# A segmented memory-attention and gated-FFN kernel: the order and the buffers of its work written out as two tables

## Chip, cores and metric

The kernel runs on one core of one Trainium2 chip. The metric is the device time of one execution in microseconds (us), lower is better. Engines are named as in the profile: PE (TensorE matmul), PEld (TensorE weight load), DVE (VectorE), ACT (ScalarE), POOL (GpSimd), SP (SyncE, which issues most DMAs).

## The reference

Inputs are bf16: `x` of 2048 tokens by 512, four 512x512 attention matrices, a 32-vector `beta`, the FFN matrices (512x1792 twice, 1792x512) and a gate vector `gate_w`. Cut to what matters:

```python
q, k, v = heads(x @ wq), heads(x @ wk), heads(x @ wv)     # 32 heads of 16, 4 segments of 512
phi = lambda t: where(t > 0, t + 1, exp(t))
mask = (ar[:, None] < ar[None, :]) * -1e9
for s in range(4):
    p = softmax(qs @ ks.T * scale + mask)
    a_dot = p @ vs
    a_mem = (phi(qs) @ M) / (phi(qs) @ z + 1e-6)
    outs.append(sigmoid(beta) * a_mem + (1 - sigmoid(beta)) * a_dot)
    M = M + phi(ks).T @ vs
    z = z + phi(ks).sum(tokens)
a = concat(outs) @ wo
b = (relu(x @ W_gate) * (x @ W_up)) @ W_down
g = sigmoid((x * gate_w).sum(-1))
return g * a + (1 - g) * b
```

## The kernel before

A program on the host builds a list of 1331 tasks. Each task (`plan.add(engine, duration, key, emit, deps, ...)`) has an engine, the tasks it depends on, the buffers it needs (`need`) and frees (`frees`), and a function `emit` that writes its instructions. After the list is built, `Plan.run` puts all tasks into one order, and the last lines of the kernel call `emit` task by task. Each engine executes its own instructions in that order; the waits between engines follow from the data and the buffers. So the order decides who waits for whom, and the assignment of buffers decides which earlier reader a writer has to wait for.

In the kernel before, `Plan.run` is a list scheduler: it keeps a model time for every engine, and at each moment starts the ready task with the smallest key whose buffers are free. The keys are formulas over the segment and chunk, to which a table `SHIFT` adds an offset for most of the 1331 tasks. `SWITCH`, `BLOCK`, `PHASE`, `FETCH`, `COLX`, `LOOK` are parameters of that model.

The work is tiled into 4 segments (`seg`) of 512 tokens, each with 4 chunks (`c`) of 8 heads; unit `u` is 4 seg + c.

- `x0_tasks` transposes the first segment's rows on PE (12 + 4 flips); the other segments' `xT` come by transposing DMAs.
- `gate_tasks(seg)` computes the token gate: four products with accumulation on DVE (the line that the trace calls L610) over the rows `xn` of that segment, an exp on ACT (`rcol`), then ratios in two layouts. `xn` is one buffer: `load_xn(seg + 1)` (issued by SP, L480) may start only when the four products of `seg` are done. For segments 1 to 3 the ratios travel through DRAM (`ratio`, `rq`, `rtok`, `rr`). For segment 0, a DVE product `q0` and a small PE matmul with a constant `fold` spread them over the partitions.
- `proj_q`, `proj_k`, `proj_v` project one chunk (matmuls of 128x512, line L663; in a form with four column tiles, L667). DVE or ACT evict each PSUM bank (`QT` L752, `ktr` L768, `Vp` L798). `proj_k` then makes `KT` (three scalings, L771), `pkT` by phi (L727, L728, after an exp on ACT, L732) and the transpose `pK` by a DMA.
- `fill_vm(seg)` copies rows of `Vp` into `Vm` by two DMAs (L807).
- `attention(seg, c)`: four groups of scores on PE (L823), each filling PSUM banks 0 to 3, one exp of 128x2048 on ACT (L845) and a triangular mask on POOL (L874); `diag` for every second chunk (L836, L856); two PV groups on PE (L896); `normalise` (transposes L927, reciprocal L935, products L937 and L932, transpose L908) into `oT`.
- `memory`, `dens`, `recall` keep and read M and z (`mbd`, `omr` L988, `coefs` and `cdr` by DMA).
- `ffn_tasks`: 14 column blocks `fv` of gate (ACT relu into `rgr`, L1047) and up (DVE product into `hT`, L1053); then `out_tile` adds W_down and wo products for 128 tokens in one bank, DVE evicts with the factor 1 - g (`osr`, L1075), SP stores. The last token tile (`tt` 15) is done in two halves of 256 columns.

Rings limit how far work runs ahead: 14 `hT`, 6 `E`, 5 `QT`/`KT`/`pqT`, 3 `ktr`, `ex1`, `rgr`, 4 `pkT`, 2 `osr`, and 8 PSUM banks.

The set-up loads (`xn` of segment 0, wq, wk, wv, gate and up in four pieces, `xT(1)`, W_down, wo, `xT(2)`) are emitted before any task, so they come first on SP in every order. wq comes in two halves of 256 columns.

The order's last step reads:

```python
    for n, d in SHIFT.items():
        plan.tasks[n].key += d
    order = plan.run()
    for t in order:
        if t.emit is not None:
            t.emit(t.col) if t.flex else t.emit()
```

Of the kernel before, what the change touches and what calls it, by code (L numbers as in the profile page):

```python
# [8 lines left out]
F32 = mybir.dt.float32  # L9
# [3 lines left out]
P = 128  # L13
S = 2048
D = 512
# [10 lines left out]
SWITCH = 105.0  # L26
BLOCK, PHASE, FETCH = 256, 191, 2950.0
COLX = 4.0
DEFER = None
LOOK = 1000.0  # L30
# [4 lines left out]
SHIFT = {  # L35
    0: -25684, 1: 1407, 2: -1330, 3: -22978, 4: -30607, 6: 36389, 7: -5637, 8: -6641, 9:
    -9156, 10: 6383, 11: -4187, 12: -13726, 13: 12497, 14: 57538, 15: -5422, 16: 1476, 17:
    -21591, 18: 23771, 19: -4129, 20: -7981, 21: 280, 22: 7068, 25: -318, 28: 21268, 29:
    -15341, 30: -57736, 31: -21028, 32: -2196, 33: -8016, 34: -783, 35: -1107, 36: -633, 38:
    15, 40: 42372, 41: 65840, 42: 5113, 43: -71216, 44: 19414, 45: 21758, 47: 5746, 50: 654,  # L40
    51: 20403, 52: 53629, 53: -20631, 54: 7059, 55: -21405, 56: -13895, 57: -740, 58: -5913,
    59: -13897, 60: 1353, 61: -40120, 62: 24385, 63: -14621, 65: 25112, 66: 3543, 67: -38939,
    69: 6399, 71: -26793, 72: -4691, 73: -2524, 75: 40537, 76: -4748, 77: -586, 80: -1662, 81:
    -105183, 82: -62163, 83: -64288, 84: 18468, 85: -40339, 86: 37103, 87: -37065, 89: 8422,
    90: 16643, 91: -13637, 92: -14487, 93: -5073, 94: 1505, 96: -1554, 97: -747, 98: -9522,
    99: -4680, 100: 4639, 101: -97803, 102: 16395, 103: 38252, 104: -69147, 105: -10415, 106:
    27259, 107: -31419, 108: 13377, 109: -123574, 111: -12785, 112: -2378, 113: 3673, 114:
    -29140, 115: 4266, 116: -62363, 117: 88, 119: -4261, 121: -33231, 122: 9814, 123: 2110,
    125: 19178, 126: 17796, 127: -23382, 128: -6689, 129: -747, 130: 22411, 131: -31402, 132:
    -16511, 133: -1373, 134: -1496, 135: 8763, 136: 29491, 137: -749, 138: 29552, 139: -20100,  # L50
    140: 44658, 141: -80409, 142: -3139, 143: -26909, 144: 1803, 145: 386, 146: 16247, 147:
    65537, 148: -3529, 149: -6241, 150: 65653, 151: 46999, 153: 14030, 154: 44020, 155: 14760,
    156: 43561, 157: -7096, 158: 45936, 159: -26024, 160: 23457, 161: 50979, 162: -46625, 163:
    -54482, 164: 88981, 165: -28687, 166: -9744, 167: 114272, 168: -31967, 169: 9267, 170:
    38917, 171: -13229, 172: 5693, 173: -28492, 174: 3768, 177: 340, 178: -26186, 179: -31211,
    181: -31531, 182: 39351, 183: -15341, 184: -100921, 185: 22252, 186: -1779, 187: -3708,
    189: -4467, 191: 37936, 192: -46874, 193: 73026, 194: -5245, 196: 16791, 197: 4743, 198:
    -45159, 199: -43211, 200: -20335, 201: 1213, 202: 125, 203: 797, 204: 8260, 205: -173671,
    206: -2254, 207: 2086, 208: -44938, 209: 42530, 210: 2685, 211: -40581, 212: 31594, 213:
    -29665, 214: -2192, 215: -61393, 217: 4901, 218: 62, 219: -31560, 220: 8015, 221: -19756,  # L60
    222: -10130, 223: -18144, 224: 68794, 225: -54104, 226: -17099, 227: 38555, 228: 53992,
    229: -20805, 230: 2476, 231: -36425, 232: -2988, 233: -4667, 234: -11209, 235: 1392, 236:
    -22096, 237: -41776, 238: -415, 239: 1533, 240: 386, 241: 10244, 242: 16354, 243: -68385,
    244: 1929, 245: -59988, 246: -4306, 247: -23793, 248: -103183, 249: -2675, 250: 35079,
    251: 580, 253: -493674, 254: -20933, 255: 697, 256: -72948, 257: -3646, 258: -15000, 259:
    2471, 260: -20761, 261: -743, 262: 7412, 263: 20962, 264: 1114, 265: -5477, 266: 29635,
    267: -95694, 268: 15975, 269: -918, 270: -11522, 271: -41685, 272: 41485, 274: -239341,
    275: -1143, 276: -1006, 277: -1966, 278: -1511, 279: -68031, 280: 21386, 281: 115009, 283:
    -13976, 285: -26218, 286: 8903, 287: 24823, 288: 3414, 289: 51471, 290: 44714, 291: 65457,
    292: -5775, 293: 23342, 294: -52538, 295: 42735, 296: 28700, 297: -891, 298: 169, 299:  # L70
    -16564, 300: -37658, 301: 52198, 302: -77259, 303: 19215, 304: 4223, 305: 38165, 306:
    173397, 307: 2166, 308: 18393, 309: 36863, 310: 1124, 311: 3176, 312: 15683, 313: -68358,
    314: 1939, 315: -10804, 316: 34, 317: -980, 318: -3471, 320: -41264, 321: -2068, 323:
    1048, 324: -899, 325: -107092, 326: 2450, 328: 543, 329: 4991, 330: 2135, 331: 32862, 332:
    11444, 333: 4290, 334: 12303, 336: 16672, 337: -8199, 338: -10438, 340: 3207, 341: 19188,
    342: 51335, 344: 41704, 345: 8287, 346: -7332, 347: 9844, 348: 72410, 349: -2946, 350:
    -4692, 351: -51689, 352: 139925, 353: 1013, 354: 37165, 355: -35242, 356: -37552, 357:
    40840, 358: -57531, 360: 338, 361: 34813, 362: -9340, 363: 15621, 365: 7805, 366: 167,
    367: -28467, 368: 3566, 369: 1686, 370: 32158, 371: -28595, 372: -13605, 373: -620, 374:
    -29762, 375: -50578, 376: -29094, 377: -4500, 378: -18438, 379: 6926, 380: -11713, 381:  # L80
    2592, 382: 28678, 384: 25379, 385: 31823, 386: 16340, 387: 17046, 388: 60789, 389: -730,
    390: 4582, 391: -15468, 392: 66683, 393: 43214, 394: 11631, 395: -22092, 396: 26488, 397:
    -65824, 398: 51325, 399: 4073, 400: 417, 401: -12246, 402: 2493, 403: 60686, 404: 33157,
    405: -9018, 406: -3996, 407: -134963, 408: -21328, 409: 1451, 410: 7686, 411: -1030, 412:
    -27724, 413: 18333, 414: 11330, 415: 8620, 416: -71493, 417: 7355, 418: 51598, 419: -8421,
    420: 7069, 421: 3185, 422: -36336, 423: 87360, 424: -6430, 425: 16914, 426: 11785, 427:
    62686, 428: 52403, 429: -14143, 430: -4565, 431: 4777, 432: -31918, 433: 11745, 434:
    10666, 435: 94, 436: 686, 437: 25603, 438: 17039, 439: -1226, 440: 1265, 441: -20575, 442:
    8235, 443: -3138, 444: -30408, 445: 5091, 446: 19491, 447: -54497, 448: -22163, 449:
    -49529, 450: 45855, 451: 6110, 452: -2600, 453: 27760, 454: 7956, 456: 14632, 457: 14498,  # L90
    458: -7407, 459: 246, 460: 54389, 461: -45592, 462: -12249, 463: 9152, 464: 7024, 465:
    8349, 466: 8939, 467: -12828, 468: -5305, 469: -28674, 470: 1790, 471: 22067, 472: 8119,
    473: 5003, 474: 1424, 475: -40794, 476: 1452, 477: 120749, 478: 4568, 480: -35928, 481:
    -5506, 482: 61504, 483: 34766, 484: -8966, 485: -17563, 487: 29633, 488: 6458, 490: 15043,
    491: 7030, 492: -15797, 493: 25921, 494: 17134, 495: 360, 496: 34064, 498: -3554, 499:
    1864, 500: -3887, 501: 59696, 502: -2935, 503: -60651, 504: -42594, 505: 213, 506: -17474,
    507: -2187, 508: 95, 509: -34011, 510: -1408, 511: 5879, 512: -203909, 513: 73486, 514:
    28663, 515: 10250, 517: 10912, 518: 10294, 520: 57556, 521: 46448, 522: 7685, 523: -830,
    524: 25912, 525: -41304, 526: 78731, 527: 56834, 528: 2389, 529: 6987, 530: -8151, 531:
    7296, 532: 457, 533: 40865, 534: 9213, 535: -7140, 536: 1038, 537: 3375, 539: -30525, 540:  # L100
    17951, 541: 3198, 542: -28519, 543: -67, 544: -8718, 545: 21976, 546: 1952, 547: 3138,
    548: -58497, 549: 38416, 550: 22607, 551: 172585, 552: 30409, 553: 19609, 554: -59594,
    555: 18272, 556: 63244, 557: 51613, 558: 18778, 560: 1285, 561: 8777, 562: 859, 563:
    64816, 564: 10753, 565: 5534, 566: 27513, 567: -666, 568: 42956, 569: -32272, 570: -2400,
    571: -34879, 572: 28274, 573: -45032, 574: 7638, 575: 1838, 576: 6680, 577: 20107, 578:
    14616, 579: -4332, 580: -28208, 581: -14633, 582: 734, 584: -32958, 585: -2694, 586: 2834,
    587: -9046, 588: 2913, 589: 46788, 590: -11636, 591: -1009, 593: -21251, 594: 3643, 596:
    -27878, 597: -2270, 598: -1189, 599: 4132, 600: 1971, 601: 56415, 602: 5034, 603: -36,
# [124 lines left out]
class Plan:  # L233
# [4 lines left out]
    def pool(self, name, n):  # L238
        for i in range(n):
            self.free[name, i] = 0.0  # L240
# [918 lines left out]
```

## Time and profile before

| what | us |
|---|---|
| median of 3 runs | 268.13 (267.17 to 269.19) |
| profiled execution | 269.25 |
| its span in the profile | 267.5 |
| PE busy | 257.2 |
| DVE busy | 198.7 |
| ACT busy | 182.5 |
| POOL busy | 57.8 |

A profile row of a timeline reads: start, duration, engine, source line, operation, output<-input, shape, how often; in brackets the idle time before it and what ended that. Matmuls overlap in the pipeline, so a group's duration is longer than the distance between starts. "SPq" rows are the issuing of a DMA on SP, not its transfer. A row of the windows reads: the stretch, its length, then busy time and count of PE, PEld, DVE, ACT and POOL, the clock, the DMA share and GB/s.

### The profile page before, as it was taken

Reading aid. Unit: us, or ns where it says so; the run is one execution under the profiler, and the core shown is the slowest. Engines: PE = TensorE matmul, PEld = TensorE weight load, DVE = VectorE, ACT = ScalarE, POOL = GpSimd, SP = SyncE. Lnnn points to the kernel's source line nnn. Section 1 sums busy time; section 2 is a strip of 40 time slices with the busy share of each in tenths; the row PEclk is TensorE's granted clock in tenths of the full one; section 3 lists DMA queues with packets and bytes.
Section 4 is the critical chain, followed back from the end, with each engine's and each line's share of the span. In section 5 each row is a group of like instructions: output and inputs, shape, how many; then the busy total and the mean of one; then the engine's idle time right before and its main releaser. Section 6 shows DMA issues by size and latency. Waiting matters only on the chain.

```text
span 267.5 us, 8524 instructions
## 1 busy us (share of the span) xinstructions
PE 257.2 (96%) x3669; PEld 120.1 (45%) x3699; DVE 198.7 (74%) x455; ACT 182.5 (68%) x168; POOL 57.8 (22%) x146
## 2 busy tenths in 40 slices
PE   8999999999998799999999999999999999999995
PEld 5444444445444244454544344534444444444554
DVE  4797889999794999896786998769782846536722
ACT  3269989999788387998498766798878786124000
POOL 7013142222321222222112231232132312000000
PEclk9999999999999999999999999999999999999999
DMA  7999981215039101200221012002200130000001
GB/s 216 349 250 341 248 191 28 86 29 104 20 66 210 36 12 35 89 14 11 45 73 51 22 23 102 30 0 56 82 2 0 32 100 22 20 0 0 5 22 61
DMA packets 32573, 20.62 MB, mean 77 GB/s; under 512 B 15000, under 2 KB 31000, under 8 KB 32536
## 3 DMA queue, kind: packets, MB, share of 16 engines
q1 hardware_dynamic: 32248, 19.82, 28.3%
q8 instruction: 29, 0.48, 0.7%
q10 hardware_dynamic: 288, 0.26, 0.3%
q14 instruction: 8, 0.07, 0.1%
HBM read 13.21 MB, written 2.55 MB: 59 GB/s over the span
## 4 chain that ended last, share of the span: by engine, by line
PE 79%; DMA 7%; DVE 5%; SPq 3%; ACT 3%; issue 2%; POOL 0%; DVEq 0%; ACTq 0%
PE ps L663 48%; PE ps L667 16%; PE ps L823 7%; PE ps L896 6%; DMA xn<-in_A_x_dram 3%; DMA wg_sb<-in_B_W_gate_dram 3%; ACT E L845 2%; SPq L470 2%; DMA pK<-pkT 1%; DVE junk L610 1%; PE ps L836 1%; PE ps L1002 1%; SPq L807 1%; DVE T L927 1%; SPq L507 0%
## 5 line engine op out<-in xcount | busy, mean ns | idle before, releaser
L845 ACT ACTIVATE E<-ps 128x2048 bf16<-128x2048 f32 x64 | 120.1, 1876 | 29.6 <-PE ps L823 23.7
L874 POOL TENSOR_SCALAR_AFFINE_SELECT E<-E 128x256 bf16<-128x256 bf16 x128 | 53.1, 438 | 169.2 <-ACT E L845 169.2
L1053 DVE TENSOR_TENSOR hT<-ps,rgr 128x512 bf16<-128x512 f32 x56 | 38.1, 686 | 19.0 <-ACT rgr L1047 12.4
L663 PE MATMUL ps<-xT,wu_sb 128*128 128x512 bf16 x194 | 50.1, 380 | 0.7 <-issue 0.6
L1047 ACT ACTIVATE rgr<-ps 128x512 bf16<-128x512 f32 x56 | 33.0, 599 | 21.7 <-PE ps L663 16.7
L663 PE MATMUL ps<-xT,wg_sb 128*128 128x512 bf16 x172 | 46.4, 380 | 0.4 <-issue 0.2
L663 PE MATMUL ps<-wd_sb,hT 128*128 128x512 bf16 x135 | 33.5, 380 | 0.9 <-issue 0.8
L927 DVE STREAM_TRANSPOSE T<-ps 128x512 f32<-128x512 f32 x32 | 21.7, 703 | 12.6 <-PE ps L896 11.5
L663 PEld LDWEIGHTS <-wu_sb 128*128 128x128 bf16 x200 | 18.4, 98 | 22.5 <-issue 1.7
L663 PEld LDWEIGHTS <-wg_sb 128*128 128x128 bf16 x180 | 16.5, 98 | 21.0 <-issue 2.7
L823 PE MATMUL ps<-QT,KT 32*128 32x320 bf16 (+3 forms) x512 | 25.4, 273 | 0.4
L1075 DVE TENSOR_SCALAR osr<-ps,ngcol 128x512 bf16<-128x512 f32 (+1 forms) x17 | 12.0, 706 | 13.9 <-PE ps L667 8.9
L667 PE MATMUL ps<-wd_sb,hT 128*32 128x512 bf16 (+1 forms) x384 | 20.4, 348 | 0.0
L663 PEld LDWEIGHTS <-hT 128*128 128x128 bf16 x142 | 12.9, 98 | 16.2 <-issue 2.3
L823 PEld LDWEIGHTS <-KT 32*128 32x128 bf16 x512 | 7.7, 92 | 26.4 <-issue 26.1
L896 PE MATMUL ps<-E,Vp 128*17 128x320 bf16 (+3 forms) x512 | 18.9, 274 | 0.0
L845 ACT ACTIVATE Em<-ps 128x2048 bf16<-128x2048 f32 x8 | 15.0, 1877 | 2.2 <-PE ps L836 2.2
L663 PE MATMUL ps<-wv_sb,xT 128*128 128x512 bf16 x60 | 16.1, 379 | 0.0
L663 PE MATMUL ps<-xT,wk_sb 128*128 128x512 bf16 x53 | 14.4, 380 | 0.7 <-issue 0.3
L610 DVE SCALAR_TENSOR_TENSOR junk<-xn,gwb 128x512 bf16<-128x512 bf16 x16 | 11.0, 688 | 3.8 <-DMA xn<-in_A_x_dram 3.8
L768 DVE CAST ktr<-ps 128x512 bf16<-128x512 f32 x16 | 10.9, 681 | 2.6 <-PE ps L663 2.6
L667 PEld LDWEIGHTS <-hT 128*32 128x32 bf16 x384 | 9.9, 97 | 6.4
(105 smaller groups left out, 294.8 us busy)
## 6 DMA issues: line engine op xcount, KB each, us to landing
cdr<-coefs SPq DMA_DIRECT2D x12, 256.0 KB
out_dram<-osr SPq DMA_DIRECT2D x15, 128.0 KB
wd_sb<-in_B_W_down_dram SPq DMA_DIRECT2D x2, 896.0 KB
xn<-in_A_x_dram SPq DMA_DIRECT2D x3, 512.0 KB
Vm<-Vp SPq DMA_DIRECT2D x8, 144.0 KB
wg_sb<-in_B_W_gate_dram SPq DMA_DIRECT2D x2, 512.0 KB
wu_sb<-in_B_W_up_dram SPq DMA_DIRECT2D x2, 512.0 KB
wg_sb<-in_B_W_gate_dram SPq DMA_DIRECT2D x2, 384.0 KB
```

Of the source, the lines that this page charges most:

```text
L610: zs.append(plan.add("DVE", 690, key, lambda t=t: nc.vector.scalar_tensor_tensor(junk[:], xn[:, t, :], 1.0, gwb[:], ALU.mult, ALU.mult, ac ...
L663: nc.tensor.matmul(out, lhsT=lhsT, rhs=rhs, start=start, stop=stop)
L667: nc.tensor.matmul(out[r], lhsT=lhsT[:, r], rhs=rhs, start=start, stop=stop, tile_position=(0, 32 * j))
L768: d = plan.add("DVE", 600, key - RQK, lambda: nc.vector.tensor_copy(ktr[ks.i][:], bank(sl)), [a], DVL + 40, need=[ks], frees=[sl])
L823: nc.tensor.matmul(ps[:, j * L + o:j * L + o + L - q], lhsT=KT[i][rows, kb, 3 * r:3 * r + 2].rearrange("p h q -> p (h q)"), rhs=QT[i][rows ...
L845: last_exp[0] = [plan.add("ACT", 66 + 4 * L / 1.2, key, lambda: nc.scalar.activation(dst, ps[:, 0:4 * L], ACT.Exp, scale=SCALE), [a] + war ...
L874: nc.gpsimd.affine_select(out=m[:, :, o:o + HP], in_=m[:, :, o:o + HP], compare_op=ALU.is_ge, fill=0.0, base=HP, pattern=[[0, 4], [1, HP]] ...
L896: nc.tensor.matmul(bank(sl)[32 * j:32 * j + HW, q:q + w], lhsT=(Vp[i] if n < 4 else Vm)[:, kb, r, 4 * c + j, 0:HW], rhs=rhs, start=(n == 0 ...
L927: done.append(plan.add("DVE", 633, key - RL, lambda r=r, sl=sl: nc.vector.transpose(T[ts.i][:, r], bank(sl)), [a] + done, 75 if r else 0, ...
L1047: r = plan.add("ACT", 478, key - RL, lambda sl=gsl, rs=rs: nc.scalar.activation(rgr[rs.i][:], bank(sl), ACT.Relu), [g], ACL, frees=[gsl])
L1053: nc.vector.tensor_tensor(hT[hs1.i][:], bank(sl), rgr[rs.i][:], ALU.mult)),
L1075: b = plan.add("DVE", 95 + 1.12 * w, key - RL, lambda: nc.vector.tensor_scalar(osr[os.i][:, 0:w], bank(sl)[:, 0:w], ngcol[:, tt:tt + 1], N ...
```

## The change

`SHIFT`, the model parameters, `link`, `pick` and the scheduling loop go. `Plan.run` takes the order from a table `ORDER` (1334 task numbers) and the buffer of every slot from a table `UNITS` (576 hexadecimal digits). Three pieces of work change as well: wq is loaded in two halves of 256 rows, and the projection of q for segment 0 is three tasks a chunk (rows of the first half for either half of the tokens, then rows of the second half); the first ratios are spread by 16 small POOL copies in four tasks instead of the DVE product and the PE matmul, and the constants `fold` and `quad` go; the second half of the last token tile is evicted half by DVE and half by ACT. The changed landing and latency numbers (`LANDS` and others) are now only annotations.

```diff
-SHIFT = {
...
-}
+ORDER = """
+    6 3 1 0 26 27 29 2 31 19 30 4 28 32 5 77 35 33 34 64 37 90 38 51 36 78 65 66 52 53 91 79 80
...
+UNITS = (
...
     def run(self):
-        users = {}
+        order = [self.tasks[int(n)] for n in ORDER.split()]
+        slots = {}
         for t in self.tasks:
...
+            for s in t.need + t.frees:
+                slots.setdefault(id(s), s)
...
+        for s, n in zip(slots.values(), UNITS):
+            s.units = s.cands[int(n, 16)]
...
     def load_q(i):
-        return load_cols(nc.sync, wq_sb, A_wq, 256 * i, 256 * i + 256, "q" + "ab"[i])
+        return load(nc.sync, wq_sb[:, 2 * i:2 * i + 2, :],
+                    A_wq.rearrange("(c p) n -> p c n", p=P)[:, 2 * i:2 * i + 2, :], "q" + "ab"[i])
...
-        if seg == 0:
-            sl, q0 = work(), sb([P, 4, 4], F32, "q0")
-            d = plan.add("DVE", 90, key, lambda: nc.vector.tensor_tensor(
-                q0[:], rcol[:, seg, None, 0:4].to_broadcast([P, 4, 4]),
-                quad[:, :, None].to_broadcast([P, 4, 4]), ALU.mult), [c], DVL, lock=True)
-            d = plan.add("PE", 260, key, lambda: nc.tensor.matmul(
-                bank(sl)[:, 0:16], lhsT=fold.rearrange("p j q -> p (j q)"),
-                rhs=q0.rearrange("p b t -> p (b t)"), start=True, stop=True), [d], PEL, need=[sl],
-                size=4)
...
+        def spread(b):
+            for j in range(4):
+                nc.gpsimd.tensor_copy(rq[0][32 * j:32 * j + 32, b], rcol[32 * b:32 * b + 32, 0, 0:4])
+        if not seg:
+            d = [plan.add("POOL", 900, key, lambda b=b: spread(b), [c], POL) for b in range(4)]
...
-        if seg == 0 and c < 2:
+        if seg == 0:
             a = None
             for h in range(2):
-                a = matmuls(key + 20000 * (h - 1), [got_q[0]], sl, [
+                a = matmuls(K(-8 + h, c), [got_q[0]], sl, [
...
-                    for ci in range(NC)], width=L // 2, at=h * L // 2, prev=a,
-                    chunk={ci: got_x[0][ci // 2] if h else x0_first for ci in range(NC)})
+                    for ci in range(2)], width=L // 2, at=h * L // 2, prev=a, start=not h, stop=False,
+                    chunk={0: got_x[0][0] if h else x0_first})
+            a = matmuls(K(-6, c), [got_q[1]] + got_x[0][1], sl, proj_mm(wq_sb, c, 0)[2:], prev=a,
+                        start=False)
...
+        both = n1 == D and tt == NT - 1
+        m = w // 2 if both else w
...
+        if both:
+            b.append(plan.add("ACT", 240, key - RL, lambda: nc.scalar.activation(
+                osr[os.i][:, m:w], bank(sl)[:, m:w], ACT.Copy, scale=ngcol[:, tt:tt + 1]),
+                [a, att["ng", seg]], DVL, frees=[sl]))
...
-    for n, d in SHIFT.items():
-        plan.tasks[n].key += d
     order = plan.run()
```

Read per engine, ORDER also moves tasks of every kind. Those that the prediction speaks of: the four products of segment 1 (L610) go from DVE places 56, 58, 62 and later to places 43, 45, 49 and 53 of 380; `load_xn(1)` becomes the first task on SP after the set-up loads (before the fourth), `fill_vm(0)` the second; `load_xn(3)` goes from SP's 20th place to its 14th, ahead of `xT(3)` and of the first `coefs` and `cdr` transfers.

## The prediction

> **What bounds the kernel now.** I read the first part of the page, then the clock row, then what PE (TensorE) waited for, then PE's own timeline to price its work, and last the places where it stood still.
>
> ```profile
> PE 257.2 (96%) x3669; PEld 120.1 (45%) x3699; DVE 198.7 (74%) x455; ACT 182.5 (68%) x168; POOL 57.8 (22%) x146
> ...
> PEclk9999999999999999999999999999999999999999
> ```
>
> PE works 96% of the 267.5 us span at an undisturbed clock. The end moves only if PE's work shrinks, if its idle time shrinks or grows, or if what follows its last matmul changes. PE's waits, summed by what ended them (total, times, longest):
>
> ```profile
> PE ps L663 <- issue: 2.9, 18, 0.2
> PE ps L667 <- DVE Vp L798: 1.9, 1, 1.9
> PE ps L1090 <- DVE mcol_e L531: 1.1, 1, 1.1
> PE ps L663 <- DMA wk_sb<-in_A_wk_dram: 0.3, 1, 0.3
> PE ps L663 <- DVE omr L988: 0.2, 1, 0.2
> ```
>
> The 18 issue waits are not idle time: the page counts 30 matmuls fewer than weight loads, and each such wait stands where a matmul's record is missing. So I price PE by the spacing of starts, from PE's timeline:
>
> ```profile
> 223.76 1.03 PE L663 MATMUL ps<-xT,wu_sb 128*128 128x512 bf16 x4
> 224.72 0.40 PE L823 MATMUL ps<-QT,KT 32*128 32x320 bf16 x8
> 225.05 1.47 PE L663 MATMUL ps<-xT,wu_sb 128*128 128x512 bf16 x6
> ...
> 236.07 1.89 PE L663 MATMUL ps<-xT,wu_sb 128*128 128x512 bf16 x8
> 237.80 1.03 PE L663 MATMUL ps<-xT,wg_sb 128*128 128x512 bf16 x4
> ```
>
> Eight 512-wide matmuls take 237.80 - 236.07 = 1.73, or 0.216 each. A score group takes 225.05 - 224.72 = 0.33, and 0.10 before it for the change of tile form (224.72 less 223.76 + 4 x 0.216). In the same way a PV group is 0.56 and a 256-wide matmul 0.109. The list of tasks has 914 x 0.2158 + 52 x 0.109 + 64 x 0.435 + 8 diagonal scores x 0.455 + 32 PV x 0.559 + 6 x 0.112 + 3 memory x 0.489 + 4.78 (warm-up, flips, junk, fold) + 1.05 before the first matmul = 260.25 us. The last matmul ends near 264.3, so PE stood still for about 4.05. After it come an eviction and a store, 3.2 to the end of the span. The two large stalls:
>
> ```profile
> 86.44 0.69 DVE L610 SCALAR_TENSOR_TENSOR junk<-xn,gwb 128x512 bf16<-128x512 bf16 x1 [3.58 <-DMA xn<-in_A_x_dram]
> ...
> 88.16 0.40 PE L667 MATMUL ps<-pqT,mbd 128*32 128x512 bf16 x4 [1.88 <-DVE Vp L798]
> ```
>
> The row before PE's is at 85.99 and lasts some 0.1, so 2.05 is lost. The Vp eviction came late only because DVE (VectorE) stands in order: ahead of it were the token gate's products (L610), which waited 3.58 for the rows of segment 3. The backlog cost PE 0.55 more at 90.1 to 91.3. The other large one is at the start:
>
> ```profile
> 8.73 1.90 PE L663 MATMUL ps<-xT,wk_sb 128*128 128x512 bf16 x7 [0.30 <-DMA wk_sb<-in_A_wk_dram]
> ```
>
> By the spacing of starts this is 0.46. Some 1.0 is spread in pieces of 0.2 or less.
>
> **The change part by part.** The PE work is the same matmuls in another order: 145 changes of form by both orders, 64 scores, 32 PV. Only the fold matmul goes (**-0.11**).
>
> *Start.* Before, 8.33 of PE's sum stands ahead of the first wk matmul, in the table 8.76 (two more 512-wide matmuls): 0.43 of the 0.46 is filled. The first q matmul stands at 5.08 instead of 5.29 and needs the same copied columns, which ACT finishes at 5.27, so 0.11 more is waited there. Net **-0.35**. The wq halves by rows move pieces of 1024 B instead of 512: in the trace's packets 46 ns against 27, so 512 x 46 against 1024 x 27 over 16 engines, 0.25 earlier. I count it at nothing, as PE reaches wk after its old landing anyway. If it came 0.25 later instead, it would cost up to 0.2.
>
> *Segment 3's rows.* By ORDER, the DVE work between the last product of segment 2 (which frees xn) and the first of segment 3 grows from 5.0 to 19.8 us, counted in row durations, and the load stands 14th on SP instead of 20th, ahead of the coefficient transfers. Against the landing of 7.7 seen here that is ample: **-2.60** (2.05 + 0.55).
>
> *Segment 1's rows.* This is what I look at hardest. The table puts these products from the 56th place on DVE to the 43rd. SP's and DVE's rows before:
>
> ```profile
> 24.50 7.20 SPq L477 DMA_TRANSPOSE xT<-in_A_x_dram  x1
> 31.87 1.37 SPq L807 DMA_DIRECT2D Vm<-Vp  x2
> ...
> 35.24 0.51 SPq L480 DMA_DIRECT2D xn<-in_A_x_dram  x1
> ...
> 45.89 0.37 SPq L480 DMA_DIRECT2D xn<-in_A_x_dram  x1
> ...
> 78.75 0.41 SPq L480 DMA_DIRECT2D xn<-in_A_x_dram  x1
> ```
> ```profile
> 39.25 0.70 DVE L610 SCALAR_TENSOR_TENSOR junk<-xn,gwb 128x512 bf16<-128x512 bf16 x1 [0.21 <-DMA xn<-in_A_x_dram]
> ```
>
> SP issues the set-up loads first in both kernels, so it is busy to 31.7. The table puts this load next, ahead of the Vm fill: issue at 31.75, landing at 31.75 + x. DVE reaches place 43 at about 33.3 and stands there. Places 43 to 55 then take 7.2: four products at 0.72, three KT scalings at 0.26, two transposes 1.30, one phi 0.74, a reciprocal 0.26, two hT at 0.60. The bank freed by place 55 is what PE's 95th task (the K projection of segment 1, second chunk) needs. PE gets there at 1.05 + 134 x 0.2158 + 16 x 0.109 + 9 score groups (3.9) + 2 PV (1.1) + 4.7 = 41.4 if nothing holds it. With 0.15 for the hand-over, PE stands still for s = 31.75 + x + 7.2 + 0.15 - 41.4 = x - 2.3. From issue to landing x was 4.0 for this load in before, 3.0 for segment 2's, 7.7 for segment 3's: s is 0.7, 1.7 or 5.4. I take 4.0, as the load stands behind a transpose that here landed at 33.5: **+1.7**. The 40 to 60 us stretch is where DVE has nothing to spare, so nothing gives it back:
>
> ```profile
> 40.00:60.00 20.00, 19.43 (x245) 8.46 (x248) 19.04 (x46) 18.50 (x19) 5.31 (x13) 1.00 0.21 49
> ```
>
> Moving the load ahead also delays what SP issues after it: the Vm fill by some 0.5, and pv of the first unit stands 1.4 earlier on PE. That wait, up to 1.1, ends before the DVE one and lies within it.
>
> *First ratios.* Sixteen copies of 32x4 on POOL replace an 0.17 DVE product and the fold. Their row is missing: from MEMSET 128x1 (0.10) to AFFINE_SELECT 128x32 (0.23) they take 1.6 to 3.7. They stand between the masks of the first two units, POOL idles 169 us, and the reader is DVE place 60, past 40 us: nothing. Without that cover a mask would be late by at most 3.7.
>
> *Last half.*
>
> ```profile
> 262.56 0.48 DVE L1075 TENSOR_SCALAR osr<-ps,ngcol 128x256 bf16<-128x256 f32 x1 [1.22 <-PE ps L667]
> ...
> 264.53 0.48 DVE L1075 TENSOR_SCALAR osr<-ps,ngcol 128x256 bf16<-128x256 f32 x1 [1.48 <-PE ps L667]
> ```
>
> 512 columns take DVE 0.736, 256 take 0.484: 128 take 0.36. ACT's rows (2048 in 1.876, 512 in 0.599) give 0.28. Side by side that is 0.36 instead of 0.48: **-0.12**; one after the other, 0.64 and a hand-over: +0.2. I take the first, as nothing in the diff orders the two. The Trainium skill, "PSUM — Partial Sum Buffer", section "PSUM bank collisions raise a hardware error", speaks against this: two engines on one bank and the same 32 partitions collide even on disjoint columns and must be ordered by a semaphore. By that rule the sum would be 0.3 worse; no row here shows two engines in one bank.
>
> *New tight places.* Between the last PV and the first matmul that needs its result the table leaves 3.67 + 0.65 of PE work, before 4.53 + 0.65, and DVE needed 3.8 (249.00 to 252.84): 0 to 0.5. From last score to PV the smallest distance falls from 5.40 to 3.46, against 1.88 of exp and 0.8 of masks: 0 to 0.3 a time. In sum 0 to 1.0; I take **+0.2**.
>
> Sum: -0.11 - 0.35 - 2.60 + 1.7 - 0.12 + 0.2 = **-1.3**. The profiled execution took 269.25 (span 267.5, 1.75 around it), 1.1 over the median of 268.13. So it becomes 267.95, and the median **266.8**.
>
> **The rivals.** *Full gain:* the rows land within 2.3, or DVE catches up: s = 0, -3.2 without the allowance, 264.9. For it: the load of segment 2 took 3.0 on a quiet queue. Against: here it follows an unfinished transpose. *Slower:* the early load of segment 1 becomes the new stall on DVE. At x = 7.7, s = 5.4 gives +2.4: 270.5. From x = 5.3 nothing is gained, from 8.0 it is over 1% slower. For it: the third load did take 7.7, and Vm fill and pK transposes now queue right behind. Against: its own 4.0 before. *It does not do what it says:* two tables that restate the same matmuls; if DVE holds PE at both places after all (the 2.6 stays) and the bank serialises, -0.11 - 0.35 + 1.7 + 0.2 + 0.2 = +1.6: 269.8.
>
> **How the numbers follow.** 1% (2.7 us) is about what a measurement of this kernel can tell from no change. Likeliest case (x from 3 to 5, so 265.8 to 267.8 by itself) 0.52; full gain 0.24; slow landing 0.16; no relief 0.08. The bound for faster is 265.45: 0.18 of the full gain lies below, and 0.07 of the likeliest case with no allowance spent: 0.25. The bound for slower is 270.81: half of the last two cases, 0.12, and 0.05 for waits of a new order that no row of before shows: 0.17. Within, 0.58. The range, 264.5 to 271.0, holds the full gain (down to 264.9) and the slow landing (270.5) with a little room on either side for what could not be priced closer.
>
> **What would show it.** Right: no DVE wait for xn near 86 us, no PE wait for wk, a DVE wait for xn at L610 near 33 us and a PE wait of 0.7 to 2.7 on a DVE eviction near 41; last eviction 0.36 beside an ACT row of 0.28. Wrong: a PE stall in another place above 1 us (a Vm fill, a mask behind the POOL copies, wo at the end), an xn wait above 5 us, or matmuls spaced wider than 0.216.

## The result and the profile after

| | before | after |
|---|---|---|
| median of 21 runs, us | 267.78 (266.49 to 270.13) | 269.95 (267.75 to 272.01) |
| profiled execution, us | 269.25 | 268.10 |
| its span, us | 267.5 | 266.4 |

The ratio is 1.0063, 95% interval 1.0040 to 1.0086 (it leaves disturbed runs out, so it is smaller than the quotient of the medians): a small loss where 1.3 us of gain was forecast. The two profiled executions say the opposite, 1.1 us less. Both are true: single executions of either kernel differ by more than the change does, and that is the first thing to explain.

PE's waits in the profile after (total, times, longest):

```profile
PE ps L678 <- DMA Vm<-Vp: 1.9, 1, 1.9
PE ps L443 <- issue: 1.4, 9, 0.2
PE ps L877 <- DVE mcol_e L327: 1.1, 1, 1.1
```

The waits for wk, for Vp and for omr are gone; in their place stands one for the Vm fill. Its place, from the timelines of SP, DVE and PE:

```profile
31.00 0.49 SPq L275 DMA_DIRECT2D xn<-in_A_x_dram  x1
31.60 1.38 SPq L589 DMA_DIRECT2D Vm<-Vp  x2
```
```profile
32.82 0.69 DVE L834 TENSOR_TENSOR hT<-ps,rgr 128x512 bf16<-128x512 f32 x1 [0.27 <-PE ps L443]
36.81 0.69 DVE L397 SCALAR_TENSOR_TENSOR junk<-xn,gwb 128x512 bf16<-128x512 bf16 x1 [3.30 <-DMA xn<-in_A_x_dram]
```
```profile
34.70 0.61 PE L678 MATMUL ps<-E,Vp 128*17 128x448 bf16 x16
37.24 0.29 PE L678 MATMUL ps<-Em,Vm 128*17 128x64 bf16 x16 [1.93 <-DMA Vm<-Vp]
...
37.79 0.61 PE L678 MATMUL ps<-E,Vp 128*17 128x448 bf16 x16
38.23 0.29 PE L678 MATMUL ps<-Em,Vm 128*17 128x64 bf16 x16
```

The rows of segment 1 take 5.8 from issue to landing, and the Vm fill behind them 5.6 from its first issue. PE loses 2.10: from 34.70 to 37.24 it takes 2.54, where the next pair of the same rows takes 0.44. DVE waits at the same time, 3.30, and is just as late: the chain of waits runs not through Vm but through the rows (L397 is the line of the products, L709 the transposes that free PE's bank; start, length, what):

```profile
31.00 5.79 DMA xn<-in_A_x_dram
36.78 0.02 issue
36.81 0.70 DVE junk L397 x2
37.51 0.27 DVE KT L553
37.78 0.61 DVE junk L397 x2
38.38 0.63 DVE T L709
39.01 0.50 DVE KT L553 x2
39.51 0.61 DVE junk L397 x2
40.12 0.64 DVE T L709
40.76 0.04 issue
40.80 1.46 PE ps L443 x6
```

So two early transfers hold two engines side by side, and taking one away should leave the other. Near 86 us, where the first profile of before lost 2.6, nothing waits.

The last eviction is not side by side. From the timeline:

```profile
263.11 0.37 ACT L862 ACTIVATE osr<-ps,ngcol 128x128 bf16<-128x128 f32 x1 [15.14 <-PE ps L447]
263.51 0.35 DVE L858 TENSOR_SCALAR osr<-ps,ngcol 128x128 bf16<-128x128 f32 x1 [1.34 <-ACT osr L862]
```

DVE starts after ACT has ended: 0.75 from the first start to the last end, where one eviction took 0.48.

### The profile page after: what moved, and what is told of

It reads as the page before. It is cut to its first block, busy times and chain, and to the rows that moved or that the text cites. A ratio compares the mean times of both kernels' runs of the same rounds, so it can differ in the third digit from the quotient of the medians.

```text
span 266.4 us, 8215 instructions
## 1 busy us (share of the span) xinstructions
PE 257.3 (97%) x3525; PEld 118.9 (45%) x3556; DVE 199.6 (75%) x447; ACT 182.9 (69%) x169; POOL 61.0 (23%) x162
## 4 chain that ended last, share of the span: by engine, by line
PE 92%; DMA 2%; issue 2%; DVE 2%; ACT 1%; ACTq 0%
PE ps L443 63%; PE ps L447 12%; PE ps L605 7%; PE ps L678 6%; DMA xn<-in_A_x_dram 2%; PE ps L618 1%; PE ps L877 1%; DVE junk L397 1%; ACT rgr L828 1%; PE ps L783 1%; PE ps L479 1%; DVE T L709 0%; PE ps L734 0%; DVE KT L553 0%; ACT osr L862 0%
## 5 line engine op out<-in xcount | busy, mean ns | idle before, releaser
L443 PE MATMUL ps<-xT,wu_sb 128*128 128x512 bf16 x204 | 54.4, 379 | 0.8 <-issue 0.5
L443 PE MATMUL ps<-xT,wg_sb 128*128 128x512 bf16 x181 | 49.5, 380 | 0.6 <-issue 0.2
L443 PE MATMUL ps<-wd_sb,hT 128*128 128x512 bf16 x139 | 37.3, 380 | 0.6 <-issue 0.3
L443 PEld LDWEIGHTS <-wu_sb 128*128 128x128 bf16 x212 | 19.8, 98 | 24.7 <-issue 2.3
L709 DVE STREAM_TRANSPOSE T<-ps 128x512 f32<-128x512 f32 x32 | 22.2, 706 | 10.4 <-PE ps L678 9.9
L443 PEld LDWEIGHTS <-wg_sb 128*128 128x128 bf16 x190 | 17.8, 98 | 21.5 <-issue 1.5
L858 DVE TENSOR_SCALAR osr<-ps,ngcol 128x512 bf16<-128x512 f32 (+2 forms) x17 | 11.8, 698 | 9.1 <-PE ps L447 6.7
L443 PE MATMUL ps<-xT,wk_sb 128*128 128x512 bf16 x61 | 17.8, 380 | 0.2
L443 PE MATMUL ps<-xT,wq_sb 128*128 128x512 bf16 (+1 forms) x67 | 16.0, 354 | 0.2 <-issue 0.2
L534 DVE CAST QT<-ps 128x512 bf16<-128x512 f32 x16 | 10.7, 678 | 4.6 <-PE ps L443 4.6
L397 DVE SCALAR_TENSOR_TENSOR junk<-xn,gwb 128x512 bf16<-128x512 bf16 x16 | 10.8, 678 | 3.3 <-DMA xn<-in_A_x_dram 3.3
```

The costliest lines, as they stand in the source:

```text
L397: zs.append(plan.add("DVE", 690, key, lambda t=t: nc.vector.scalar_tensor_tensor(junk[:], xn[:, t, :], 1.0, gwb[:], ALU.mult, ALU.mult, ac ...
L443: nc.tensor.matmul(out, lhsT=lhsT, rhs=rhs, start=start, stop=stop)
L534: prj["q", seg, c] = plan.add("DVE", 600, key - RQK, lambda: nc.vector.tensor_copy(QT[i][:], bank(sl)), [a], DVL, frees=[sl])
L709: done.append(plan.add("DVE", 633, key - RL, lambda r=r, sl=sl: nc.vector.transpose(T[ts.i][:, r], bank(sl)), [a] + done, 75 if r else 0, ...
L858: b = [plan.add("DVE", 95 + 1.12 * m, key - RL, lambda: nc.vector.tensor_scalar(osr[os.i][:, 0:m], bank(sl)[:, 0:m], ngcol[:, tt:tt + 1], ...
```

## The experiments

Three theories. *Early transfers:* the new order makes PE and DVE wait for rows and Vm fill near 35 us, by an amount that differs between executions. *Unusual profile:* the loss near 86 us that the prediction took back was mostly not there in a typical execution of before. *Clock:* a pause of PE lowers its clock afterwards, which costs more than the pause. Every run comes with its span and its granted clock, and the theories differ in what they expect of them. The runs lie on several chips; before was run beside each and has medians of 267.69 to 267.86 there.

**The changed kernel again**, unchanged.

> The changed kernel again, unchanged, for its spread and a second profile. Early-transfer theory: the two transfers that SP issues right after the set-up loads (rows of segment 1, then the Vm fill) land late by a different amount in every execution; the profile again shows PE waiting about 2 us (1.5 to 4) on the Vm fill near 35 us, and the runs scatter over 2 us, 267.7 to 270.5, at one and the same clock. Clock theory: the runs above 269.5 are those with a granted clock of 0.991 to 0.995, and at clock 1.0 the kernel takes 268.1 and is level with before or faster.

Median 269.06 (12 runs), ratio 1.0039 (1.0010 to 1.0069). The profile shows the same place:

```profile
PE ps L678 <- DMA Vm<-Vp: 1.7, 1, 1.7
```

With the 21 runs before it there are 33: in 19 the clock is 0.998 to 1.0, and their spans go from 265.8 to 268.7, median 267.0; in 14 it is 0.991 to 0.994, spans 267.8 to 270.3, median 268.55. The early-transfer theory and the clock theory hold together: a spread of 2.9 us at one clock, and 1.5 more in the median where the clock is lower. Of 97 runs of before whose clock is known, 3 are below 0.997.

**Vm fill ahead of the rows** on SP.

> Only the first two SP tasks exchanged: Vm fill, then the rows of segment 1. Early-transfer theory: the Vm fill is issued at 31.0 and lands in 2.5 us as in before (2.45), so PE's wait of 2.15 near 35 us goes; but the rows then land 1.4 us later (near 38), DVE waits 4.7 instead of 3.3, and PE waits 2 to 3.5 us on a DVE eviction (fv10) before the K projection at 41 us: total 0 to 1.3 us slower than the changed kernel. Theory that the Vm fill alone is at fault and DVE has slack: 2 us faster than the changed kernel.

```diff
 ORDER = """
-... 42 43 358 339 24 100 123 414 15 44 115 89 359 ...
+... 42 43 358 24 100 123 414 15 44 115 339 89 359 ...
```

Median 270.75 (9 runs), ratio 1.0096 (1.0066 to 1.0126): slower, as expected of two waits side by side, though 1.7 over the changed kernel beside it (269.06) is more than the 0 to 1.3 expected. PE no longer waits for Vm, but for DVE's transposes (two waits, 2.5 in all), which stand behind rows that land later. The Vm fill lands 3.6 after its first issue. That is what it took in before too (31.87 to 35.48 by the landing records: the trace keeps 16 reports for the landing of a load, and the last one counts; the 2.45 of the expectation is about the time to the first report). Four of the nine runs have a lower clock (0.987 to 0.994), and the profile caught one of them. Windows of it (busy time of PE, PEld, DVE, ACT, POOL, then the clock, the DMA share and GB/s):

```profile
38.00:40.00 2.00, 0.31 (x8) 0.13 (x9) 2.00 (x6) 1.78 (x2) 0.00 (x0) 1.00 0.00 0
40.00:42.00 2.00, 1.31 (x4) 0.44 (x4) 2.00 (x6) 0.30 (x1) 1.57 (x3) 0.70 0.01 4
42.00:44.00 2.00, 1.85 (x5) 0.69 (x5) 1.97 (x7) 0.00 (x0) 1.90 (x4) 0.50 0.03 8
44.00:46.00 2.00, 2.00 (x17) 0.66 (x15) 0.98 (x3) 1.01 (x1) 0.00 (x0) 0.95 0.49 170
```

PE is busy 0.31 of two microseconds, and then for some 3.4 us its clock is half: 0.6 + 1.0 + 0.1 = 1.7 us of clock are lost, which is the 0.994 of the whole span.

**Vm first, and the products late.** ORDER as above, and the four products of segment 1 moved to DVE places 55 to 65 (the load of the next rows, which needs them done, moves back on SP with them).

> Vm fill before the rows of segment 1 on SP, and the four products of segment 1 moved from places 43 to 53 on DVE to places 58 to 65, as late as in before. Early-transfer theory: both waits go, PE does not stop between 31 and 45 us; 1.5 to 2.3 us faster than the changed kernel, in the profile a span near 264.3, and the scatter of the runs at clock 1.0 falls below 1 us. Clock theory: still runs at 0.993 with 1.6 us more than those at 1.0.

Median 268.48, ratio 1.0008 (0.9981 to 1.0036): 0.6 to 1.3 better than the changed kernel (269.06 beside it, 269.74 of the 33), less than the 1.5 to 2.3 expected, as Vm still lands late (PE waits 0.4) and the moved products now delay a Vp eviction:

```profile
PE ps L678 <- DVE Vp L580: 1.3, 1, 1.3
PE ps L678 <- DMA Vm<-Vp: 0.4, 1, 0.4
```

None of its 12 runs has a clock under 0.998, and the spans keep within 1.5 us. So the products in a late place trade one wait for another; whether the late transfers are the cause is for the next run.

**The transposing load of segment 2 later.** It is a set-up load that holds SP for 7 us. Its first reader is PE's 167th task, a V projection of segment 2, at 74.93 in the profile after, so the "80 us" of the expectation is somewhat late.

> The transposing load of segment 2, which holds SP from 23.9 to 30.9 and is not read before 80 us, is issued after the first four pK transposes instead of with the set-up loads; the order is otherwise that of the changed kernel. Early-transfer theory: the rows of segment 1 are issued near 28 and land by 32, the Vm fill lands by 33.5, neither DVE nor PE waits for them; 1.8 to 2.5 us faster than the changed kernel, span near 264.2. If the transfers are late for another reason than SP's queue (the 16 DMA engines still busy with the set-up loads), the wait of PE on Vm stays at 1 us or more.

```diff
-    load_xT(2)
     got_x[2] = [[arrival("x2")]] * 2
-    plan.add("SP", 31700, -1e9, None)
+    plan.add("SP", 31700, -1e9, lambda: load_xT(2))
```

Median 266.13, ratio to before 0.9935 (0.9912 to 0.9958); a second time 266.30, 0.9941 (0.9920 to 0.9963), expected as

> The variant with the later transposing load, unchanged, beside the one above. Early-transfer theory: again 266.0 to 266.5, no run with a granted clock under 0.996, spans within 1.2 us of each other; no PE wait above 0.5 us after the start.

It beats both kernels. SP's timeline:

```profile
24.62 0.79 SPq L275 DMA_DIRECT2D xn<-in_A_x_dram  x1
25.52 2.12 SPq L588 DMA_DIRECT2D Vm<-Vp  x2
27.69 2.14 SPq L565 DMA_TRANSPOSE pK<-pkT  x1
39.66 0.39 SPq L275 DMA_DIRECT2D xn<-in_A_x_dram  x1
40.10 5.61 SPq L565 DMA_TRANSPOSE pK<-pkT  x3
45.75 2.66 SPq L272 DMA_TRANSPOSE xT<-in_A_x_dram  x1
```

Both transfers leave SP 6 us earlier and nothing waits for them (in the second profile DVE does, 0.4). They land only 3.1 earlier: by the landing records the rows at 33.69 instead of 36.79 and the first part of Vm at 34.10 instead of 37.20, just before DVE (33.71) and PE ask for them. So the change to SP's queue pays, but half of the time gained at the issue is spent behind the loads that still lie ahead. The load's hold on SP and its traffic were moved together; which of them delayed the rows was not separated. The 21 spans lie between 263.8 and 265.3, median 264.4, none under a clock of 0.997. That is what the new order is worth without its early wait: 1.6 less than before's median span of 266.0.

**The same in the kernel before.** There the load is issued after the last of the first five pK transposes.

> The kernel before with the transposing load of segment 2 issued after the fourth pK transpose instead of with the set-up loads. Early-transfer theory: in this order nothing waits for the rows of segment 1 or the Vm fill for more than 0.3 us, so it is no gain here, within 0.5 us of before. If SP's early queue costs every order something, it gains 1 us or more.

267.57, ratio 0.9992 (0.9955 to 1.0028): no difference within 0.4%, as expected. SP's late queue costs the order that asks for rows and Vm early, and not this one.

**The kernel before, a second profile.**

> The kernel before again, for a second profile. The first profiled execution took 269.25, 1.1 over its median. Theory that this one was unusual: the rows of segment 3 now land in 4.5 to 6.5 us instead of 7.7, PE's stall near 86 us is 0.3 to 1.4 instead of 2.05, and the span is near 266.0 instead of 267.5. Theory that the stall is always there and the excess lies elsewhere: again 2 us near 86, and less somewhere else.

266.57, span 264.9. From DVE's timeline:

```profile
83.44 0.69 DVE L610 SCALAR_TENSOR_TENSOR junk<-xn,gwb 128x512 bf16<-128x512 bf16 x1 [0.95 <-DMA xn<-in_A_x_dram]
```

The load issued at 78.38 lands in 5.1, not 7.7, DVE waits 0.95 instead of 3.58, and PE does not wait for it. What the stall cost can now be read off two score groups of PE, in the first profile and in the second:

```profile
84.67 0.40 PE L823 MATMUL ps<-QT,KT 32*128 32x448 bf16 x8
92.71 0.40 PE L823 MATMUL ps<-QT,KT 32*128 32x320 bf16 x8
```
```profile
84.30 0.40 PE L823 MATMUL ps<-QT,KT 32*128 32x448 bf16 x8
89.92 0.40 PE L823 MATMUL ps<-QT,KT 32*128 32x320 bf16 x8
```

8.04 against 5.62: 2.42 of the 2.6 by which the spans differ. Of the 94 runs of before at full clock, 22 have spans from 267.0 to 269.2 and the others 264.8 to 266.9, median 266.0. So neither profile is typical: 267.5 belongs to the longest quarter, and 264.9 is as short as the shortest three. The median lies 1.1 above the profile without the stall and 1.5 below the one with it.

**The kernel before, segment 3's products later on DVE.**

> The kernel before with one thing of the new order: the first three products of segment 3 stand 15 to 18 places later on DVE (after some 10 us more of its work), so that nothing on DVE waits for the rows. What the prediction counted: 2.6 us faster (ratio 0.990). Unusual-profile theory: the typical execution loses only about 1 us there, so 0.7 to 1.5 us faster (ratio 0.995 to 0.997), and spans at 264.5 to 265.5. Nothing on PE between 80 and 95 us waits for DVE.

```diff
     order = plan.run()
+    dve = [t for t in order if t.eng == "DVE"]
+    for z, n in ((2, 151), (0, 154), (1, 158)):
+        t = att["xn", 3][z]
+        order.remove(t)
+        order.insert(order.index(dve[n]) + 1, t)
```

268.36, ratio 1.0009 (0.9982 to 1.0036). The longest runs are gone (12 spans from 265.7 to 267.2, where 9 of the 29 of before beside them are 267.4 or more), but the typical one is 0.6 longer (266.6 against 266.0). Neither the 2.6 of the prediction nor the 1 us of the rival theory is there to be had by this step alone. What the later products cost in exchange was not found; PE has a new wait of 0.3 for DVE's hT, at 94.7.

**PE kept busy in the wait.** The changed kernel with 1.9 us of matmuls that add zero, between the Vp and the Vm matmuls of the first PV group.

> The changed kernel with 10 rounds of 4 matmuls with zero weights (1.9 us of PE work that adds zero to the first PV bank) put where PE waits for the Vm fill. Clock theory: PE is busy through most of the wait, so the clock is not lowered after it; runs with a granted clock under 0.996 fall from about 15 of 33 to at most 1 of 10, and the median falls by 0.5 to 1.2 us against the changed kernel although PE has 1.9 us more work (to 268.3 to 268.9). If the lower clock has nothing to do with the wait, the share of such runs stays near a half, and the median rises by 0 to 0.5 us.

```diff
                 for n in range(8):
+                    for k in range(4 * NJ if (u, r, n) == (0, 0, 4) else 0):
+                        nc.tensor.matmul(bank(sl)[32 * (k % 4):32 * (k % 4) + HW, HP:L], lhsT=nil[:],
+                            rhs=Er[0][:, 0:L - HP], start=False, stop=False, tile_position=(0, 32 * (k % 4)))
```

None of 12 runs is under 0.998, where it was 14 of 33. In time nothing can be told: the median is 269.2, between the 269.06 and the 269.95 of the changed kernel's two groups, and the ratio to before 1.0041 (1.0009 to 1.0072). In its profile the rows come only at 38.3 and PE still waits 0.7 for Vm. So the busy PE kept its clock; what that saved and what the 1.9 us of added work cost can't be told apart here.

**A pause of PE with no transfer in it**, in the variant with the later load, once near 36 and once near 84 us: a matmul that adds zero, six POOL memsets of its weights, and another.

> The variant with the later transposing load, and in the first PV group of unit 0 (near 35 us, where the changed kernel waits for the Vm fill) a pause of PE that has nothing to do with a DMA: a matmul with zero weights, six POOL memsets of those weights (about 2 us), a second such matmul (0.4 us of PE work in all, and a wait of about 2.2). Theory that a pause of PE by itself lowers the clock: 3 to 6 of 10 runs show a granted clock of 0.990 to 0.995 and take 1.6 us more than the rest; the rest take 2.2 to 2.6 us more than the variant without (266.2), 268.4 to 268.8. Theory that late transfers and the lower clock only come together: no run under 0.996.

> The same pause in the first PV group of unit 4, near 84 us, about where the kernel before has its stall for the rows of segment 3. If a pause anywhere lowers the clock as often as near 35 us: again 3 to 6 of 10 runs at 0.990 to 0.995. By the kernel before, in which 13 of 56 runs at full clock have lost 2 us or more and only 2 of 58 show a lower clock, at most 1 of 10. The rest take 2.2 to 2.6 us more than 266.2.

```diff
+                    for k in range(2 if (u, r, n) == (PU, 0, 4) else 0):
...
+                        for m in range(6 * (1 - k)):
+                            nc.gpsimd.memset(nil[:], 0.0)
```

Both profiles show one wait of 2.3. Near 36 us 6 of 12 runs have a clock of 0.991 to 0.994 (median 270.7, the other six 269.6); near 84 us 5 of 8 (270.5, the other three 269.9). Of the 21 runs without the pause none is under 0.997. By the kernel before, the second pause should have lowered the clock at most once in ten: it did so as often as the first, so the place is not what matters. Its profile is one of the five, PE's timeline after the pause:

```profile
86.40 0.37 PE L675 MATMUL ps<-E,nil 128*17 128x448 bf16 x4 [2.29 <-POOL nil L680]
86.59 0.37 PE L688 MATMUL ps<-Em,Vm 128*17 128x64 bf16 x16
86.76 1.91 PE L446 MATMUL ps<-wd_sb,hT 128*32 128x512 bf16 x16
88.45 1.07 PE L688 MATMUL ps<-E,Vp 128*17 128x448 bf16 x16
```

Sixteen matmuls that take 0.87 at full clock take 88.45 - 86.76 = 1.69. In full-clock runs the pause costs 3.3 and 3.6 rather than the 2.2 to 2.6 expected. With its two matmuls it delays PE by 2.9 in the profile near 36 us (Vp group to Vm group 3.34, less 0.44); where the rest goes was not found.

**One engine for the last half**, in the variant with the later load.

> The variant with the transposing load of segment 2 issued later, and the last 256 columns evicted by DVE alone as in before. In the profiles of the new order DVE's half begins only when ACT's has ended (0.37, then 0.35). If that is a wait and not chance, one eviction of 0.48 replaces 0.75 from the last matmul: the span is 0.25 to 0.3 shorter, time 265.7 to 266.0. If the two engines work side by side in typical executions, it is 0.1 longer: 266.2.

```diff
-        m = w // 2 if both else w
+        m = w
...
-            b.append(plan.add("ACT", 240, key - RL, lambda: nc.scalar.activation(
...
+            b.append(plan.add("ACT", 240, key - RL, None,
```

266.27 against 266.30 of its neighbour, 0.9950 (0.9927 to 0.9973) against 0.9941: inconclusive in the time. In the profile the eviction is one row of 0.48 again, where the variant with two engines has 0.37 and 0.35 one after the other as in the changed kernel; 0.27 is less than what the runs vary by.

## Why the prediction was wrong

**"Against the landing of 7.7 seen here that is ample: -2.60."** This term failed first, by its size. The wait does disappear, but the median execution of before holds less of it than the profiled one, and the forecast was made for the median. The prediction saw that its profiled execution was 1.1 over the median and carried the 1.1 through as a constant, when by the two profiles of before the difference lies almost wholly in the very stall that it took back (2.42 of 2.6). Its sum without the +1.7 is -3.0; without the early wait the new order is worth 1.6 (264.4 against 266.0), which is 1.4 less. About 0.4 of that would be the last eviction by its rows (below), and the 1.0 that is left is about what the profiled execution lay over the median. That the median execution of before waits some 1.1 there, and not 2.6, fits this but is not shown: none of that length was profiled.

**"I take 4.0, as the load stands behind a transpose that here landed at 33.5: +1.7."** The wait was foreseen in its place and kind, and mis-sized: x was 5.8. It was not the transpose that made it longer: its last report came at 33.72 here, and at 35.24 in before (33.5 was the first of its 16). The landing records of the rows show where the time went: 15 of the 16 reports come by 35.33, the last at 36.79 (35.56 and 37.02 in the second profile of the changed kernel). With 15 reports x would have been 4.3. Segment 3's rows in before show the same: 15 reports by 82.31 and the last at 86.42 in the first profile, 82.43 and 83.42 in the second. Up to the 15th report x is 3.6 to 4.3 in all of these, so its spread is mostly the lag of one report out of 16; what holds that one was not found. In the two profiles with the later transposing load the last report on these rows comes at most 0.3 after the one before it.

The formula did not fit either: s = x - 2.3 gives 3.5, and 2.4 was lost in this execution (2.10 and 0.28 at 40.80). The load was issued at 31.00 and not 31.75, and the DVE places behind it took 6.6 (36.81 to 43.39) and not 7.2, so s at the K projection would have been 2.1; PE, held up before by 2.4, came there at 43.82 and did not wait any more. In the median full-clock run the early wait costs 267.0 - 264.4 = 2.6, so +1.7 was 0.9 too small.

**"That wait, up to 1.1, ends before the DVE one and lies within it."** Issued 0.5 later, the Vm fill was thought to be late by at most 1.1. With 512 KB of rows ahead of it, it landed 5.6 after its issue, PE lost 2.10 on it, and it ended at 37.24, after DVE's wait (36.81). It cost nothing on top in this execution, as the chain through the rows is 0.28 longer. But the pause of PE came of it, and so, in part of the executions, the next term.

**No term for the clock.** "PE works ... at an undisturbed clock" was read off one execution of before and kept for the new order. 14 of 33 executions of the changed kernel have a lowered clock, and those take 1.3 us more in the median (1.5 in the span); with PE kept busy in the wait it was none of 12. The rule that pauses over some 3 us are to be avoided stands in the Trainium skill, "TensorE: Matmul & The Clock Gate", section "Why this matters for your kernels"; here 2.3 us were enough in 11 of 20 runs.

**"-0.12; one after the other, 0.64 and a hand-over: +0.2. I take the first, as nothing in the diff orders the two."** They come one after the other: DVE's row waits for ACT's, 0.75 in all where one eviction took 0.48, +0.27. The bank rule cited there asked for just this order. In the time of the runs the 0.27 could not be seen.

With these: -1.6 + 2.6 and 14 of 33 times about 1.4 more is +1.6 in the mean; the medians of the 33 and the 97 differ by 269.74 - 267.80 = 1.9. (The first two numbers are 267.0 - 266.0 in two steps, so only the clock's share is tested by this sum.) Against the -1.3 of the prediction that is 3.2: 1.4 from the gain, 0.9 from the early wait, 0.6 from the clock, and 0.3 left over.

**Right:** the start (wk begins at 8.76 with no wait), the fold, the POOL copies (3.0 in the estimate's 1.6 to 3.7, nobody waits for them), no xn wait near 86, a DVE wait for xn from 33.5. "Slower: the early load of segment 1 becomes the new stall" was the rival that came true, at x = 5.8 rather than 7.7; its price went wrong by the clock and by the gain that it was set against. That the profiled execution of after came out 1.1 below the one of before, near the forecast -1.3, was luck: a short execution of the one beside a long one of the other. The wq halves by rows were not tried alone.

## What to carry to other kernels

A stall that one profile shows is worth what it takes over many executions: before taking it back, see a second profile, and if the profiled run lies above the median, suspect the stall. When a load is moved to the front of a queue, price everything that the queue issues behind it with the load's bytes ahead of it, and look for what holds the queue (here a 7 us transposing load that nobody needed for over 40 us). A pause of PE can cost its length and, here in 14 of 33 and 11 of 20 executions, a half-speed stretch after it: read the clock of every run, not only of the profiled one.

## What was not expected of the hardware

A pause of 2.3 us on PE, with no transfer in it, lowered the clock in 11 of 20 executions, in the profiled one for about 3.4 us at half; waits of 1.9 and 0.6 for DVE did it too, in the profile of the Vm fill ahead of the rows. That before lowered its clock in only 3 of 97 runs, though a fifth of them (19 of 94 at full clock) are 1.4 us or more over the median, stays open. The length of the pause alone does not explain it: the 1.88 that PE waits in the first profile of before is no shorter than the 1.7 to 1.9 in the two of the changed kernel, none of which lowered the clock, and no execution of the changed kernel with a lowered clock was profiled.

The landing of a load can hang on one report out of 16: 4.1 us after the one before it for segment 3's rows in the first profile of before, 1.0 in the second.
